# V in its own tile with 320-byte rows and two ones columns, one more free weight buffer: a one-core transformer block

## The chip, the cores and the metric

One core of one Trainium2 chip runs the kernel. The metric is device time in microseconds. Each time quoted is a median of several executions unless it is said otherwise. Ratios with 95% intervals: the mean time of one kernel's fast runs over that of the other's of the same rounds, so not quite the ratio of the medians quoted beside them.

In the profiles TensorE is PE (its weight loads PEld), VectorE is DVE, ScalarE ACT, GpSimd POOL; SP issues transfers. SBUF and PSUM are on-chip memories: this kernel's matmuls read tiles in SBUF and write tiles in PSUM. The granted clock is the share of its full clock that TensorE got, as the trace records it; "half clock" is a record of 0.5.

Below, a "start-to-start" time is the time from the start of one matmul to the start of the next, taken from the starts recorded in the trace. It matters because successive matmuls overlap: in before the profile gives an o_ps 219 ns on average, and the next one starts 57.8 ns after it.

## The reference

A block of 2048 tokens with D = 1024: adaptive layer norm, attention of 32 query heads over 4 cached K/V heads (the last 512 keys of each, head width 128), a residual, adaptive layer norm, a SwiGLU FFN of width 3584, a residual. Cut to what matters here:

```python
W = min(4096, max(256, Sk // 4))                      # 512
k = jnp.repeat(k_cache[:, :, Sk - W:, :], rep, axis=1)
v = jnp.repeat(v_cache[:, :, Sk - W:, :], rep, axis=1)
scores = jnp.einsum('bhqd,bhkd->bhqk', q, k) * Dh ** (-0.5)
p = _softmax(scores, axis=-1)
o = jnp.einsum('bhqk,bhkd->bhqd', p, v)
...
x = x + ga * _A_ref(h, A_k_cache, A_v_cache, A_wq, A_wo)
...
x = x + gb * _B_ref(h, B_w_gate, B_w_up, B_w_down)
```

## The kernel before

V lies in SBUF as 4 heads x 4 key blocks, each block a row of 128 values and some ones behind them. The matmul that makes the attention output reads 129 columns of such a row: 128 of V, and a column of ones whose product is the softmax denominator. A row takes 132 values, so 264 bytes. The tile comes from the pool that also holds wq, wg and wu, and stays there until attention ends.

```python
pa_ = ctx.enter_context(tc.tile_pool(name="blkA", bufs=8))
pb_ = ctx.enter_context(tc.tile_pool(name="blkB", bufs=7))     # wq, wg, wu; before: also kT and V
pc_ = ctx.enter_context(tc.tile_pool(name="blkC", bufs=13))    # wo, wd, oq, oT
# ... cut ...
VW = Dh + 4
v_sb = blkB("v_sb", [P, Hkv, WT, VW])
for kv in range(Hkv):
    load(v_sb[:, kv, :, 0:Dh], v_v[:, kv])
nc.gpsimd.memset(v_sb[:, :, :, Dh:VW], 1.0)
# ... cut ...
def emit_o(g):
    # ... cut ...
    for t in range(QT):
        if o_slot["n"] == 0:
            o_slot["ps"] = mm("o_ps", (P, SLOTS, Dh + 1))
        s_ = o_slot["n"]
        for j in range(WT):
            nc.tensor.matmul(o_slot["ps"][:, s_, :], lhsT=pT[g][:, j, t * P:(t + 1) * P],
                             rhs=v_sb[:, kv, j, 0:Dh + 1], start=(j == 0),
                             stop=(j == WT - 1))
```

There are 128 heads and token chunks, with 16 such matmuls each: 2048 in all. Around them run the 512-column matmuls q_ps (queries), s_ps (scores) and a_ps (output projection). After attention come gu_ps (gate and up) and d_ps (down) of the FFN. Nearly all loads and the transposes by DMA are issued in order from one queue (SP).

Of the kernel before, what the change touches and what calls it, by code (L numbers as in the profile page):

```python
# [11 lines left out]
BF16 = mybir.dt.bfloat16  # L12
# [576 lines left out]
def fast_path(ctx, tc, flag, A_x, A_k_cache, A_v_cache, A_wq, A_wo, B_x, B_w_gate, B_w_up,  # L589
# [3 lines left out]
    nc = tc.nc  # L593
    P = 128
    _, S, D = A_x.shape
    _, Hkv, Sk, Dh = A_k_cache.shape
# [11 lines left out]
    WT = W // P  # L608
# [20 lines left out]
    const = ctx.enter_context(tc.tile_pool(name="const", bufs=1))  # L629
# [1 line left out]
    hpool = ctx.enter_context(tc.tile_pool(name="hT", bufs=4))  # L631
    pa_ = ctx.enter_context(tc.tile_pool(name="blkA", bufs=8))
    pb_ = ctx.enter_context(tc.tile_pool(name="blkB", bufs=7))
    pc_ = ctx.enter_context(tc.tile_pool(name="blkC", bufs=13))
    wk = ctx.enter_context(tc.tile_pool(name="work", bufs=2))
    sm = ctx.enter_context(tc.tile_pool(name="small", bufs=4))
    psp = ctx.enter_context(tc.tile_pool(name="psum", bufs=4, space=bass.MemoryType.PSUM))
# [5 lines left out]
    def blkB(name, shape, dt=BF16):  # L643
        return pb_.tile(shape, dt, name=name, tag="B")

    def blkC(name, shape, dt=BF16):
        return pc_.tile(shape, dt, name=name, tag="C")

    def mm(name, shape=(P, 512), dt=FP32):
        return psp.tile(list(shape), dt, name=name, tag="mm", bufs=4)  # L650
# [15 lines left out]
    def load(out, in_):  # L666
        with nc.allow_non_contiguous_dma(reason="weight slice"):
            fetch(out=out, in_=in_)
# [20 lines left out]
    def load_wq(cc, hg, parts=(0, 1)):  # L689
        for i in parts:  # L690
            t = blkB("wq", [P, 4, 512])
            load(t, wq_v[:, 4 * i:4 * i + 4, hg * 512:(hg + 1) * 512])
            wq_tiles[(cc, hg, i)] = t
# [8 lines left out]
    for kv in range(Hkv):  # L702
        pin(nc.sync.dma_start_transpose(
            out=kT[:, kv, :], in_=A_k_cache[0, kv, k0:k0 + W, :]), "dma")
    VW = Dh + 4
    v_sb = blkB("v_sb", [P, Hkv, WT, VW])
    for kv in range(Hkv):
        load(v_sb[:, kv, :, 0:Dh], v_v[:, kv])
    nc.gpsimd.memset(v_sb[:, :, :, Dh:VW], 1.0)
    load_wq(0, 1)  # L710


# [218 lines left out]
    for half in range(DH):  # L931
# [6 lines left out]
        for n in range(4 * LEAD):  # L938
# [3 lines left out]
                             rhs=hT[("h1", 0)][:, dt, :], start=(dt == 0), stop=(dt == DT - 1))  # L942
# [96 lines left out]
    SLOTS = 3  # L1039
    o_slot = {"n": 0, "runs": []}  # L1040

    def close_bank():
        ps, runs = o_slot["ps"], o_slot["runs"]
        n = o_slot["n"]
        rl = sm.tile([P, SLOTS], FP32, name="rl", tag="rl", bufs=4)
        nc.vector.reciprocal(out=rl[:, 0:n], in_=ps[:, 0:n, Dh])
        for g, t0, t1, s0 in runs:
            cnt = t1 - t0
            dst = oq[(g // H, (g % H) // 4)][:, t0:t1, g % 4, :]
            sc = rl[:, s0:s0 + cnt].unsqueeze(2).to_broadcast([P, cnt, Dh])  # L1050
            nc.vector.tensor_tensor(out=dst, in0=ps[:, s0:s0 + cnt, 0:Dh], in1=sc, op=ALU.mult)  # L1051
        o_slot.update(n=0, runs=[])

    def emit_o(g):
        cc, h = divmod(g, H)
        kv = h // rep
        if h % 4 == 0:
            oq[(cc, h // 4)] = blkC("oq", [P, QT, 4, Dh])
        for t in range(QT):
            if o_slot["n"] == 0:  # L1060
                o_slot["ps"] = mm("o_ps", (P, SLOTS, Dh + 1))
            s_ = o_slot["n"]
            for j in range(WT):
                nc.tensor.matmul(o_slot["ps"][:, s_, :], lhsT=pT[g][:, j, t * P:(t + 1) * P],  # L1064
                                 rhs=v_sb[:, kv, j, 0:Dh + 1], start=(j == 0),
                                 stop=(j == WT - 1))
            runs = o_slot["runs"]
            if runs and runs[-1][0] == g:
                runs[-1][2] = t + 1
            else:  # L1070
                runs.append([g, t, t + 1, s_])
            o_slot["n"] = s_ + 1
            if o_slot["n"] == SLOTS or (t == QT - 1 and h % HQ == HQ - 1):
                close_bank()
        del pT[g]
# [127 lines left out]
    for k in range(NU + 1):  # L1203
        if k % 4 >= 2 and 4 * (k // 4) + 8 < NU:
            g = 4 * (k // 4) + 8
            load_wq(g // H, (g % H) // 4, (k % 4 - 2,))
        if k < NU:
            emit_s(k)
        if k + LEAD < NU:
            emit_q(k + LEAD)  # L1210
        if k == NU - 4:
            load_gu(0, 0)
        run_tasks(k)
        if k >= 1:
            emit_o(k - 1)
# [20 lines left out]
def kernel(tc, *args):  # L1236
    nc = tc.nc
    with tc.tile_pool(name="guard", bufs=1) as gp:
        flag = gp.tile([1, 1], I32, name="flag")
        fast_path(tc, flag, *args)  # L1240
        over = nc.values_load(flag[0:1, 0:1], min_val=0, max_val=1)
        with tc.If(over > 0):
            general_path(tc, *args)
# [30 lines left out]
```

## Time and profile before

| | before |
|---|---|
| time | 1287.03 us, median of 3 (1285.96 to 1289.07) |
| span of the profiled run | 1287.8 us, mean granted clock 0.996 |
| TensorE busy | 1272.8 us, 99% |
| o_ps, sum of start-to-start times | 118.4 us for 2048 matmuls, 57.8 ns each |
| 512-column matmuls, start-to-start | 215 to 216 ns |

From the profile's page of before: the busy times, the granted clock in 40 slices (9 is 90% or more), the chain of waits by engine and by line, and the group of o_ps (busy us and mean ns of one, then idle time before).

```profile
span 1287.8 us, 18140 instructions
...
PE 1272.8 (99%) x7601; PEld 644.0 (50%) x7601; DVE 577.8 (45%) x1271; ACT 334.0 (26%) x433; POOL 1.3 (0%) x8
...
PEclk9999999999999999999999999999999999999999
...
PE 95%; DMA 2%; DVE 1%; SPq 1%; ACT 0%; issue 0%; DVEq 0%
...
L1064 PE MATMUL o_ps<-v_sb,pT 128*128 128x129 bf16 x2048 | 139.2, 219 | 0.0
```

TensorE is the limit, and nearly all of the chain of waits is TensorE's own work. The 139.2 us of the last line is not what o_ps costs, because the runs of o_ps overlap with their neighbours. The timeline of TensorE shows the cost (start, length, count):

```profile
600.48 1.09 PE L1064 MATMUL o_ps<-v_sb,pT 128*128 128x129 bf16 x16
601.41 1.02 PE L1032 MATMUL s_ps<-qT,kT 128*128 128x512 bf16 x4
602.27 1.03 PE L1019 MATMUL q_ps<-hT,wq 128*128 128x512 bf16 x4
```

Sixteen o_ps begin at 600.48 and the next group begins at 601.41: 0.93 us, or 58 ns each. The four s_ps of 512 columns take 0.86 us, or 215 ns each.

Broken down by the key block j, the start-to-start times in the trace are 56.1, 59.9, 55.9 and 59.4 ns for j = 0 to 3.

Three lines of the view of waits matter (total us, times, longest):

```profile
DVE modT L802 <- DMA modT<-row_d: 3.6, 1, 3.6
...
PE gu_ps L1168 <- DMA wu<-in_B_w_up_dram: 2.1, 1, 2.1
...
PE a_ps L1096 <- DVE acc L1102: 1.0, 1, 1.0
```

The first and the third are one story, near 92 us: VectorE stands still until the small modulation transfer lands, so a copy out of PSUM behind it is late, and TensorE waits for that copy. The second is at 756 us, and the timeline shows what follows it:

```profile
755.16 1.03 PE L1168 MATMUL gu_ps<-hT,wu 128*128 128x512 bf16 x4
...
758.26 1.04 PE L1168 MATMUL gu_ps<-hT,wu 128*128 128x512 bf16 x4 [2.08 <-DMA wu<-in_B_w_up_dram]
...
759.14 3.16 PE L1168 MATMUL gu_ps<-hT,wg 128*128 128x512 bf16 x8
```

Eight gu_ps normally take 1.89 us from first start to last end. The eight at 759.14 take 3.16 us. The trace's record of the granted clock gives half clock from 759.6 us for 3.41 us.

### The profile page before, as it was taken

Reading aid. Unit: us, or ns where it says so; the run is one execution under the profiler, and the core shown is the slowest. Engines: PE = TensorE matmul, PEld = TensorE weight load, DVE = VectorE, ACT = ScalarE, POOL = GpSimd, SP = SyncE. Lnnn points to the kernel's source line nnn. Section 1 sums busy time; section 2 is a strip of 40 time slices with the busy share of each in tenths; the row PEclk is TensorE's granted clock in tenths of the full one; section 3 lists DMA queues with packets and bytes.
Section 4 is the critical chain, followed back from the end, with each engine's and each line's share of the span. In section 5 each row is a group of like instructions: output and inputs, shape, how many; then the busy total and the mean of one; then the engine's idle time right before and its main releaser. Section 6 shows DMA issues by size and latency. Waiting matters only on the chain.

```text
span 1287.8 us, 18140 instructions
## 1 busy us (share of the span) xinstructions
PE 1272.8 (99%) x7601; PEld 644.0 (50%) x7601; DVE 577.8 (45%) x1271; ACT 334.0 (26%) x433; POOL 1.3 (0%) x8
## 2 busy tenths in 40 slices
PE   7999999999999999999999999999999999999998
PEld 4555555555555555555554444444444444444444
DVE  4464557866577755576663641221122121222122
ACT  3543334343333433333341111011100111011100
POOL 0000000000000000000000000000000000000000
PEclk9999999999999999999999999999999999999999
DMA  9878465456345654445578475453536445354401
GB/s 295 264 196 221 169 148 171 133 144 203 96 123 156 148 140 147 116 147 131 132 186 257 134 218 171 135 192 132 179 103 219 152 152 175 135 192 132 147 18 34
DMA packets 280107, 204.20 MB, mean 159 GB/s; under 512 B 113865, under 2 KB 273609, under 8 KB 280018
## 3 DMA queue, kind: packets, MB, share of 16 engines
q1 hardware_dynamic: 275106, 198.78, 52.2%
q10 hardware_dynamic: 4912, 4.20, 1.0%
q8 instruction: 61, 1.00, 0.3%
q14 instruction: 28, 0.23, 0.1%
HBM read 174.08 MB, written 4.21 MB: 138 GB/s over the span
## 4 chain that ended last, share of the span: by engine, by line
PE 95%; DMA 2%; DVE 1%; SPq 1%; ACT 0%; issue 0%; DVEq 0%
PE gu_ps L1168 29%; PE a_ps L1096 17%; PE q_ps L1019 17%; PE d_ps L1188 15%; PE o_ps L1064 9%; PE s_ps L1032 8%; DMA wm<-in_w_mod_dram 1%; SPq L664 1%; DMA modT<-row_d 0%; DMA hT<-xn 0%; DMA wu<-in_B_w_up_dram 0%; PE row_ps L779 0%; PE q_ps L940 0%; DVE st L816 0%; SPq L848 0%; ACT pT L1034 0%
## 5 line engine op out<-in xcount | busy, mean ns | idle before, releaser
L1034 ACT ACTIVATE pT<-s_ps 128x1024 bf16<-128x1024 f32 x256 | 248.6, 1020 | 345.4 <-PE s_ps L1032 345.4
L1096 PE MATMUL a_ps<-wo,oT 128*128 128x512 bf16 x1024 | 241.9, 379 | 1.0 <-DVE acc L1102 1.0
L1019 PE MATMUL q_ps<-hT,wq 128*128 128x512 bf16 x1000 | 237.3, 380 | 0.3 <-DVE modT L755 0.3
L1168 PE MATMUL gu_ps<-hT,wu 128*128 128x512 bf16 x896 | 212.3, 380 | 2.1 <-DMA wu<-in_B_w_up_dram 2.1
L1168 PE MATMUL gu_ps<-hT,wg 128*128 128x512 bf16 x896 | 212.9, 381 | 0.0
L1174 DVE TENSOR_TENSOR guT<-gu_ps,sg 128x512 bf16<-128x512 f32 x112 | 77.4, 691 | 285.5 <-ACT sg L1173 285.5
L1173 ACT ACTIVATE sg<-gu_ps 128x512 bf16<-128x512 f32 x112 | 66.9, 597 | 492.6 <-PE gu_ps L1168 492.6
L1188 PE MATMUL d_ps<-wd,guT 128*128 128x512 bf16 (+2 forms) x952 | 194.2, 366 | 0.0
L916 DVE CAST qT<-q_ps 128x512 bf16<-128x512 f32 x128 | 88.2, 690 | 179.0 <-PE q_ps L1019 176.8
L1096 PEld LDWEIGHTS <-oT 128*128 128x128 bf16 x1024 | 99.9, 98 | 122.3 <-issue 2.1
L1019 PEld LDWEIGHTS <-wq 128*128 128x128 bf16 x1000 | 97.9, 98 | 117.9 <-issue 0.5
L1064 PEld LDWEIGHTS <-pT 128*128 128x128 bf16 x2048 | 128.4, 97 | 30.6 <-issue 0.4
L1188 PEld LDWEIGHTS <-guT 128*128 128x128 bf16 x952 | 90.9, 98 | 103.0
L1168 PEld LDWEIGHTS <-wu 128*128 128x128 bf16 x896 | 87.8, 98 | 108.7 <-DMA wu<-in_B_w_up_dram 2.6
L1168 PEld LDWEIGHTS <-wg 128*128 128x128 bf16 x896 | 87.9, 98 | 106.1 <-issue 1.1
L1064 PE MATMUL o_ps<-v_sb,pT 128*128 128x129 bf16 x2048 | 139.2, 219 | 0.0
L1032 PE MATMUL s_ps<-qT,kT 128*128 128x512 bf16 x512 | 131.3, 378 | 0.6 <-ACT pT L1034 0.6
L1051 DVE TENSOR_TENSOR oq<-o_ps,rl 128x256 bf16<-128x256 f32 (+2 forms) x256 | 101.3, 420 | 4.3
L1192 DVE TENSOR_TENSOR f<-d_ps,gb_bc 128x512 f32<-128x512 f32 (+2 forms) x34 | 22.4, 660 | 147.1 <-PE d_ps L1188 147.1
L1104 DVE TENSOR_TENSOR acc<-a_ps,acc 128x512 f32<-128x512 f32 x64 | 44.1, 688 | 40.8 <-PE a_ps L1096 40.8
L1032 PEld LDWEIGHTS <-kT 128*128 128x128 bf16 x512 | 44.7, 97 | 31.9 <-issue 1.3
L816 DVE BATCH_NORM_STATS2 st<-x 128x6 f32<-128x512 bf16 x64 | 41.3, 680 | 2.7 <-DMA x<-in_A_x_dram 2.5
(75 smaller groups left out, 306.7 us busy)
## 6 DMA issues: line engine op xcount, KB each, us to landing
wq<-in_A_wq_dram SPq DMA_DIRECT2D x64, 512.0 KB, 4.8
wo<-in_A_wo_dram SPq DMA_DIRECT2D x64, 512.0 KB, 5.5
wg<-in_B_w_gate_dram SPq DMA_DIRECT2D x56, 512.0 KB, 5.0
wu<-in_B_w_up_dram SPq DMA_DIRECT2D x56, 512.0 KB, 5.6
wd<-in_B_w_down_dram SPq DMA_DIRECT2D x56, 512.0 KB, 7.2
wmr<-in_w_mod_dram SPq DMA_DIRECT2D x8, 1024.0 KB, 8.6
x<-in_A_x_dram SPq DMA_DIRECT2D x16, 256.0 KB, 5.1
wm<-in_w_mod_dram SPq DMA_DIRECT2D x4, 1024.0 KB, 10.7
```

Of the source, the lines that this page charges most:

```text
L916: nc.vector.tensor_copy(out=t, in_=q_ps)
L1019: nc.tensor.matmul(q_ps, lhsT=wq_tiles[(cc, h // 4, dt // 4)][:, dt % 4, (h % 4) * P:(h % 4 + 1) * P], rhs=hT[("h1", cc)][:, dt, :], start ...
L1032: nc.tensor.matmul(s_ps[:, i, :], lhsT=kT[:, kv, j * P:(j + 1) * P], rhs=qT[g], start=True, stop=True)
L1034: nc.scalar.activation(out=p[:, 2 * jj:2 * jj + 2, :], in_=s_ps, func=ACT.Exp, scale=scale)
L1051: nc.vector.tensor_tensor(out=dst, in0=ps[:, s0:s0 + cnt, 0:Dh], in1=sc, op=ALU.mult)
L1064: nc.tensor.matmul(o_slot["ps"][:, s_, :], lhsT=pT[g][:, j, t * P:(t + 1) * P], rhs=v_sb[:, kv, j, 0:Dh + 1], start=(j == 0), stop=(j == W ...
L1096: nc.tensor.matmul(a_ps, lhsT=oT[(cc, 2 * q + i)][:, hh % 4, t * P:(t + 1) * P], rhs=wo_tiles[(cc, q, dh, i)][:, hh % 4, :], start=(hh == ...
L1104: nc.vector.tensor_tensor(out=acc[(cc, t)][:, dsl], in0=a_ps, in1=acc[(cc, t)][:, dsl], op=ALU.add)
L1168: nc.tensor.matmul(ps[:, n, :], lhsT=gu_w[(cc, fg, nm, dt // 4)][:, dt % 4, fi * P:(fi + 1) * P], rhs=hT[("h2", cc)][:, dt, :], start=(dt ...
L1173: nc.scalar.activation(out=g, in_=ps[:, 0, :], func=ACT.Silu)
L1174: nc.vector.tensor_tensor(out=guT[(cc, fg)][:, fi, :], in0=ps[:, 1, :], in1=g, op=ALU.mult)
L1188: nc.tensor.matmul(d_ps, lhsT=guT[(cc, f // 4)][:, f % 4, t * P:(t + 1) * P], rhs=wd_tiles[(cc, dh, f // 4)][:, f % 4, c0:c0 + w], start=( ...
```

## The change

V gets a tile of its own, outside the pool of wq, wg and wu, whose seven buffers are then all for weights and kT. Rows grow from 264 to 320 bytes. The matmul reads 130 columns, the second ones column being unused, so that the count is even. To make room the pool of wo and wd goes from 13 to 12 buffers.

```diff
-    pc_ = ctx.enter_context(tc.tile_pool(name="blkC", bufs=13))
+    pc_ = ctx.enter_context(tc.tile_pool(name="blkC", bufs=12))
 ...
-    VW = Dh + 4
-    v_sb = blkB("v_sb", [P, Hkv, WT, VW])
+    VN = Dh + 2
+    v_sb = const.tile([P, Hkv, WT, Dh + 32], BF16, name="v_sb")
     for kv in range(Hkv):
         load(v_sb[:, kv, :, 0:Dh], v_v[:, kv])
-    nc.gpsimd.memset(v_sb[:, :, :, Dh:VW], 1.0)
+    nc.gpsimd.memset(v_sb[:, :, :, Dh:VN], 1.0)
 ...
-                o_slot["ps"] = mm("o_ps", (P, SLOTS, Dh + 1))
+                o_slot["ps"] = mm("o_ps", (P, SLOTS, VN))
 ...
-                                 rhs=v_sb[:, kv, j, 0:Dh + 1], start=(j == 0),
+                                 rhs=v_sb[:, kv, j, 0:VN], start=(j == 0),
```

## The prediction

> **What bounds the kernel now.** TensorE. The page gives PE 1272.8 us busy of a 1287.8 us span (99%), granted clock 0.9 or more in all 40 slices; the chain that ended last is 95% PE, 9% of it the line of o_ps (attention probabilities times V). By start-to-next-start of successive matmuls in the trace, a 512-column matmul takes 215 to 216 ns everywhere, and the 2048 o_ps matmuls (129 columns) take 118.4 us in all, 57.8 ns each. PE idles at the start (about 30 us), 1.2 us near 92 us, and near 756 us, where gu_ps waits 2.2 us for a wu transfer and then runs some nine matmuls at half rate.
>
> **What I think the change aims at.** The 57.8 ns is a mean of two values. By the key block j (four in each accumulation), the trace has 56.1, 59.9, 55.9 and 59.4 ns for j = 0, 1, 2, 3. V rows are now 264 bytes apart, so odd j start 8 bytes past a multiple of 16, and even j on one. The PSUM slot makes no difference (57.8 in all three). [...] the trace fits a cost of 3.7 ns for a row that starts in mid-line. Rows of 320 bytes[...] take that away.
>
> **Costs.**
> - Removed: 1024 odd-j matmuls x 3.7 ns = 3.8 us.
> - Added: one column in 2048 matmuls. [...]
> - Net: o_ps 57.8 -> 56.4 ns each, 118.4 -> 115.4 us, about -2.9 us, all of it on PE and so on the critical path.
> - Moved: V leaves the wq/wg/wu pool, so during attention wq has six buffers instead of five. No q_ps matmul waits for wq in the trace, so this is worth nothing directly. The other weight pool has 12 instead of 13; wo and wd are loaded far enough ahead. The order of PE's instructions is the same in both; of the transfers, only a few around the start of the FFN move, and the transposes of hT still stand before the late wu, so I expect the 756 us stall to stay.
>
> **Prediction.** 1287.0 - 2.9 = 1284.1 us; range 1281.8 to 1286.6. Chances: faster by over 2% 0.01, within 2% 0.98, slower by over 2% 0.01.
>
> **What would show it.** o_ps start-to-start near 56.4 ns for all four j, no alternation; the o_ps share of the chain about 2.9 us shorter; 512-column matmuls unchanged; the FFN's start about 2.9 us earlier and the FFN's length equal; the waits for wu near 756 us as before.
>
> **What would make it wrong.** If the alternation comes from the odd column count rather than from the start, the gain still comes, by the even count. [...] The stall near 756 us, or the half-clock stretch after it, may fall differently: up to 4 us either way. One buffer less for wo and wd could hold the single in-order load queue and bring a new wait of some us. The three runs of before differ by 3 us, as much as the gain.

The 3.7 ns is an estimate from the trace of before: 59.9 and 59.4 ns for odd j against 56.1 and 55.9 ns for even j. "In mid-line" and "16-byte line" are words for a start off and on a multiple of 16 bytes. That 16 bytes is the step was assumed then; the runs below test it.

## More of the kernel before

One more piece plays a part. A late column of the modulation is fetched by a small transfer, and VectorE adds 1 to it as soon as it is there:

```python
def load_cols(n, k, dst, add_one):
    # ... cut ...
        fetch(out=dst, in_=src)
    if add_one:
        nc.vector.tensor_scalar(out=dst, in0=dst, scalar1=1.0, scalar2=None, op0=ALU.add)
```

The view of stretches, cut at four landmarks: the first o_ps, the 513th (a quarter of attention), the last, and the first d_ps. The length is the first figure after the colon, then busy times by engine, the granted TensorE clock, DMA share and GB/s.

```profile
0.00:31.57 31.57, 24.90 (x229) 12.52 (x230) 14.83 (x46) 12.22 (x20) 1.26 (x8) 0.95 1.02 293
31.57:186.58 155.01, 154.02 (x1133) 84.89 (x1132) 81.77 (x197) 63.98 (x73) 0.00 (x0) 1.00 0.73 206
186.58:677.40 490.82, 490.82 (x3400) 270.72 (x3399) 325.19 (x778) 190.91 (x229) 0.00 (x0) 1.00 0.52 144
677.40:798.81 121.41, 119.33 (x548) 53.63 (x546) 52.32 (x100) 16.12 (x27) 0.00 (x0) 0.99 0.62 189
798.81:1287.83 489.02, 483.77 (x2297) 222.28 (x2295) 103.69 (x153) 50.75 (x85) 0.00 (x0) 1.00 0.43 142
```

In the third stretch TensorE is busy for all of its 490.82 us. The others hold waits.

## The result, and the profile after

| | before | after |
|---|---|---|
| median | 1286.64 us (6 runs, 1285.78 to 1289.07) | 1287.17 us (6 runs, 1284.57 to 1287.59) |
| ratio | | 0.9997, 95% interval 0.9984 to 1.0010 |
| span of the profiled run | 1287.8 us | 1282.7 us |
| o_ps, start-to-start, sum | 118.4 us | 116.1 us |

The times are the same within noise, although the two profiled runs differ by 5.1 us. The six times of after fall into two groups, 1284.6 and 1284.8 us against 1287.1 to 1287.6, and the profile fell on the first. A pair of profiles taken alone would have told a wrong story.

From the page of after, then its view of waits, then the timeline of TensorE at the same place in the program:

```profile
span 1282.7 us, 18139 instructions
...
PE 1269.7 (99%) x7601; PEld 642.9 (50%) x7601; DVE 577.8 (45%) x1271; ACT 333.9 (26%) x433; POOL 1.2 (0%) x8
...
L1064 PE MATMUL o_ps<-v_sb,pT 128*128 128x130 bf16 x2048 | 137.1, 220 | 0.0
```

```profile
DVE modT L802 <- DMA modT<-row_d: 3.4, 1, 3.4
...
PE gu_ps L1168 <- DMA wu<-in_B_w_up_dram: 2.1, 1, 2.1
...
PE a_ps L1096 <- DVE acc L1102: 0.7, 1, 0.7
```

```profile
597.26 1.07 PE L1064 MATMUL o_ps<-v_sb,pT 128*128 128x130 bf16 x16
598.16 1.03 PE L1032 MATMUL s_ps<-qT,kT 128*128 128x512 bf16 x4
```

Sixteen o_ps now take 0.90 us, or 56 ns each. By j, the start-to-start times are 56.7, 56.7, 56.7 and 56.7 ns: the alternation is gone. Note that the group's mean duration on the page rose, from 219 to 220 ns, while the cost fell.

The same five stretches of after:

```profile
0.00:30.37 30.37, 25.43 (x229) 13.56 (x230) 14.84 (x46) 12.23 (x20) 1.23 (x8) 0.94 1.02 287
30.37:184.61 154.24, 153.51 (x1133) 84.43 (x1132) 81.69 (x197) 63.97 (x73) 0.00 (x0) 1.00 0.77 210
184.61:673.91 489.30, 489.30 (x3401) 269.36 (x3399) 325.23 (x778) 190.85 (x229) 0.00 (x0) 1.00 0.55 146
673.91:793.65 119.74, 117.64 (x548) 53.20 (x546) 52.34 (x100) 16.12 (x27) 0.00 (x0) 1.00 0.62 183
793.65:1282.70 489.05, 483.77 (x2297) 222.32 (x2295) 103.72 (x153) 50.75 (x85) 0.00 (x0) 1.00 0.45 143
```

The 5.1 us come from four places: 1.20 us in the start, 0.77 us in the first quarter of attention, 1.52 us in the rest of it, and 1.67 us at the entry to the FFN. Only the third is a stretch without waits in either kernel. In the last of the four, the wait for wu is there as before, but no half clock follows it:

```profile
754.79 1.04 PE L1168 MATMUL gu_ps<-hT,wu 128*128 128x512 bf16 x4 [2.10 <-DMA wu<-in_B_w_up_dram]
...
755.66 0.59 PE L1168 MATMUL gu_ps<-hT,wg 128*128 128x512 bf16 x2
```

The record of the clock in after's trace has one half-clock stretch in the run's body, 14.0 to 17.4 us. It falls on h_ps and warm_ps (eight h_ps took 1.01 us there and 0.62 us at 9.80 us), in front of a wait for modulation weights, which still lasted 0.35 us there, against 1.37 us in before. In before one fell on q_ps (22.3 us) and one on gu_ps (759.6 us).

What decides where the half clock falls is not shown. In before the wait of 2.08 us for wu was followed by half clock 1.3 us after its end; in after the wait of 2.10 us was not. So the length of the wait does not decide it alone in this pair, and no run was made to test what does.

### The profile page after: what moved, and what is told of

Same layout as the page of the kernel before. It is cut to its first block, busy times and chain, and to the rows that moved or that the text cites. A ratio compares the mean times of both kernels' runs of the same rounds, so it can differ in the third digit from the quotient of the medians.

```text
span 1282.7 us, 18139 instructions
## 1 busy us (share of the span) xinstructions
PE 1269.7 (99%) x7601; PEld 642.9 (50%) x7601; DVE 577.8 (45%) x1271; ACT 333.9 (26%) x433; POOL 1.2 (0%) x8
## 4 chain that ended last, share of the span: by engine, by line
PE 95%; DMA 2%; DVE 1%; SPq 1%; ACT 0%; issue 0%; DVEq 0%
PE gu_ps L1168 29%; PE a_ps L1096 17%; PE q_ps L1019 17%; PE d_ps L1188 15%; PE o_ps L1064 9%; PE s_ps L1032 8%; DMA wm<-in_w_mod_dram 1%; SPq L664 1%; DMA hT<-xn 0%; DMA modT<-row_d 0%; DMA wu<-in_B_w_up_dram 0%; PE row_ps L779 0%; PE q_ps L940 0%; DVE st L816 0%; SPq L848 0%; ACT pT L1034 0%
## 5 line engine op out<-in xcount | busy, mean ns | idle before, releaser
L1064 PE MATMUL o_ps<-v_sb,pT 128*128 128x130 bf16 x2048 | 137.1, 220 | 0.0
L1032 PEld LDWEIGHTS <-kT 128*128 128x128 bf16 x512 | 44.9, 98 | 31.7 <-issue 1.3
```

The source lines that it names most:

```text
L1032: nc.tensor.matmul(s_ps[:, i, :], lhsT=kT[:, kv, j * P:(j + 1) * P], rhs=qT[g], start=True, stop=True)
```

## The experiments

Twelve runs. Theory A is that the rows' gain is real and about 2 us, and is hidden by waits on transfers and by where half-clock stretches fall. Theory B is that something in the change, the smaller wo/wd pool above all, takes the gain back. A rival inside theory A is that the odd column count, not the row start, caused the alternation.

This table gathers what the traces gave (us). The columns are: o_ps in all; the time of the first o_ps; the first quarter of attention; the rest of attention; last o_ps to first d_ps.

| run | rows, columns | o_ps | first | quarter | rest | entry |
|---|---|---|---|---|---|---|
| before | 264, 129 | 118.4 | 31.6 | 155.0 | 490.8 | 121.4 |
| after | 320, 130 | 116.1 | 30.4 | 154.2 | 489.3 | 119.7 |
| a1_again | 320, 130 | 116.1 | 31.6 | 155.4 | 489.3 | 119.5 |
| a2_pitch_129 | 320, 129 | 116.1 | 31.5 | 154.9 | 489.3 | 119.4 |
| a3_130_only | 264, 130 | 118.4 | 31.5 | 155.0 | 490.8 | 119.2 |
| a4_pools_only | 264, 129 | 118.4 | 29.6 | 155.1 | 490.8 | 119.5 |
| c1_before_steady | 264, 129 | 118.3 | 31.3 | 155.3 | 490.8 | 118.1 |
| c2_after_steady | 320, 130 | 116.1 | 31.7 | 155.4 | 489.3 | 118.2 |
| e1_after_nowait | 320, 130 | 116.1 | 31.2 | 153.4 | 489.3 | 120.0 |
| e2_before_nowait | 264, 129 | 118.3 | 30.7 | 153.8 | 490.8 | 118.0 |

The fifth stretch, first d_ps to the end, is 488.9 to 489.1 us in all of them. In the first six rows, take TensorE's wait near 92 us (0.7 to 1.9 us) off the quarter: 154.0 us are left in each of the three kernels with 264-byte rows, 153.5 us in each of the three with 320. Take the wait for wu (1.6 to 2.1 us), and in before the 1.7 us lost at half clock, off the entry: 117.6 us are left in all six. So beyond the rows' 2.0 us these profiles differ only in the start, in the two waits and in the half clock.

### The changed kernel again

No edit.

> The changed kernel, unaltered, once more, for the spread. Its six runs fell into two groups (two at 1284.6 to 1284.8 us with a granted clock of 0.998, four at 1287.1 to 1287.6 with 0.995 to 0.997). Theory A (the o_ps gain of 2.3 us is real, and stretches of about 3.4 us of half clock fall either on a wait or on dense matmuls, at the start and after the wait near 752 us): every run with clock 0.998 has a span near 1283, every run with 0.996 near 1285.5, and before, at equal clock, is about 2 to 3 us longer. Theory B (the smaller wo/wd pool gives the gain back): at equal clock, before and after are equal.

Measured: 1286.52 us, median of 5 (1285.13 to 1287.15), ratio 0.9994 with an interval of 0.9981 to 1.0007. The granted clock alone does not sort the runs: 0.998 goes with spans of 1283.4, 1284.8 and 1285.4 us, so theory A in that form is too simple. Its profile shows what else varies. The wait near 92 us was 1.9 us here, against 0.7 in the first profile of the same kernel:

```profile
DVE modT L802 <- DMA modT<-row_d: 4.5, 1, 4.5
...
PE a_ps L1096 <- DVE acc L1102: 1.9, 1, 1.9
```

So the first quarter took 155.4 us, longer than before's 155.0, although its o_ps were faster.

### Padded rows, 129 columns

```diff
-    VN = Dh + 2
+    VN = Dh + 1
```

> The changed kernel with 129 columns in place of 130; 320-byte rows stay. [...] If the odd count is the cause: the alternation returns for odd j, o_ps near 57.8 ns and 118.4 us. Time: [...]after plus 2.3 us.

What was expected if the row start is the cause was no alternation, and a little less time because of one column less.

Measured: o_ps 116.06 us, 56.7 ns for every j. That is the same as with 130 columns to the hundredth of a us. The time was 1286.38 us, median of 6 (1284.65 to 1290.22), ratio 0.9999 (0.9985 to 1.0012). The alternation does not need 130 columns to go away, and the small gain expected for one column less did not come: an odd 129 costs what 130 costs (116.06 us both).

### 264-byte rows, 130 columns

```diff
-                o_slot["ps"] = mm("o_ps", (P, SLOTS, Dh + 1))
+                o_slot["ps"] = mm("o_ps", (P, SLOTS, Dh + 2))
-                                 rhs=v_sb[:, kv, j, 0:Dh + 1], start=(j == 0),
+                                 rhs=v_sb[:, kv, j, 0:Dh + 2], start=(j == 0),
```

> The kernel before with 130 columns only, rows still 264 bytes. Start theory: odd j still 3 to 4 ns slower than even j[...]. Odd-count theory: 56.7 ns for all j, 116.1 us.

Measured: 56.1, 59.9, 55.8 and 59.4 ns for j = 0 to 3, 118.36 us in all, as in before. The time was 1286.65 us, median of 4, ratio 0.9994 (0.9980 to 1.0009). The odd count is refuted as the cause. The second ones column is neither a gain nor a cost, here too (118.36 us with 130 columns and with 129). The view of one line's instructions tells these kernels apart by the shortest duration (min/median/max in ns), first this run, then a2_pitch_129:

```profile
L1064 PE MATMUL o_ps<-v_sb,pT x2048: 217/220/230, 31.5 to 677.3; 128*128 128x130 bf16 x187
```

```profile
L1064 PE MATMUL o_ps<-v_sb,pT x2048: 220/220/231, 31.5 to 675.7; 128*128 128x129 bf16 x187
```

Durations of 217 ns exist, in these runs, only where rows start off a multiple of 16 bytes (264 bytes, and the 258 below); with 272 and 320 bytes the shortest is 220 ns. The costlier stream has the shorter minimum, so this view shows that the two differ, not which is cheaper.

### The buffers alone

```diff
-    pc_ = ctx.enter_context(tc.tile_pool(name="blkC", bufs=13))
+    pc_ = ctx.enter_context(tc.tile_pool(name="blkC", bufs=12))
-    v_sb = blkB("v_sb", [P, Hkv, WT, VW])
+    v_sb = const.tile([P, Hkv, WT, VW], BF16, name="v_sb")
```

> The kernel before with V in its own tile and the wo/wd pool at 12, rows still 264 bytes and 129 columns: the move of the buffers alone. Theory A: o_ps as before (57.8 ns), and no new wait of PE: the time of before at equal clock, within 0.5 us. Theory B (the pool gives back what the rows gain): 2 to 3 us longer than before at equal clock, with a wait of PE for wo, wd or wu that before does not have.

Measured: 1285.68 us, median of 5 (1284.78 to 1286.05), ratio 0.9989 (0.9976 to 1.0002). Theory B wanted this to be 2 to 3 us longer than before; it is not. It came out about 1 us below before, more than the 0.5 us that theory A allowed, though within noise. It also came out 0.8 us below a1_again (1286.52 us), which has the same buffers and padded rows: timings of the kernels as they are do not show the gain of the rows. Its profile has no half clock before the end and the earliest first o_ps of all (29.6 us). Its quarter, rest and entry are those of 264-byte kernels. One short wait of q_ps for wq near 28.7 us (0.52 us) is new.

### The disturbances taken out, first try: a failure

Fillers in the start, the +1 emitted later, pools 8 and 12 (for the changed kernel 8 and 11).

```diff
-        warm(2)
+        warm(6 if t == 1 else 2)
 ...
         mod_cols(1, half, ca1, True)
+        if half == 1:
+            warm2_ps = big("warm2_ps")
+            for _ in range(6):
+                tc.keep_in_program_order(nc.tensor.matmul(
+                    warm2_ps[:, 0, :], lhsT=ones_bf, rhs=warm_w, start=True, stop=True))
         mod_cols(0, half, sa, False)
 ...
-        if add_one:
-            nc.vector.tensor_scalar(out=dst, in0=dst, scalar1=1.0, scalar2=None, op0=ALU.add)
+    def cols_add_one(dst):
+        nc.vector.tensor_scalar(out=dst, in0=dst, scalar1=1.0, scalar2=None, op0=ALU.add)
 ...
+    at(24, cols_add_one, cb1)
 ...
-    pb_ = ctx.enter_context(tc.tile_pool(name="blkB", bufs=7))
+    pb_ = ctx.enter_context(tc.tile_pool(name="blkB", bufs=8))
```

> The kernel before, with the disturbances around it taken out: warm-up matmuls fill TensorE's waits at the start, the +1 that waits for a small transfer is emitted eight steps later (the wait near 92 us), and the wq/wg/wu pool has 8 buffers, the wo/wd pool 12 (the wait near 756 us). Rows of 264 bytes, 129 columns. If half-clock stretches and these waits are what spreads the times: no stretch of half clock after 25 us, no wait over 0.5 us after 32 us, a spread of its runs under 1.5 us, and a time 3 to 5 us below before. If they are not: the time and the spread of before.

> The changed kernel with the same edits (pools 8 and 11). Theory A (the rows' gain is real and was hidden by where stretches of half clock and the wait near 92 us fall): 2.0 us less than the steadied before, from 1.5 us in the last three quarters of attention and 0.5 us in the first. Theory B (something in the changed kernel takes the gain back): the two within 0.7 us of each other.

Measured: 1287.11 us (1286.14 to 1288.06) for the 264-byte one and 1285.65 us (1285.27 to 1286.56) for the padded one, each a median of 5; ratios to before 1.0002 and 0.9991. The difference of the means is 1.3 us in favour of the padded rows, between the two theories. The expected gain over before did not come:

- The +1 still ran in front of the copy out of PSUM, although the program emits it later. In the padded one VectorE still waited 4.28 us for the transfer, and TensorE 1.06 us behind it.
- A new wait appeared near 109 us in both (0.6 us in the view of the padded one).
- The pools did their part: the wait for wu was gone from both, and the entry took 118.1 and 118.2 us. Yet the time of the 264-byte one did not fall.
- The fillers did not start attention earlier: first o_ps at 31.3 and 31.7 us. The last modulation weights arrived at about 21.3 us in the first of them, as late as in after, the rest of the start comes behind that transfer, and q_ps then waited 0.6 us for wq. One of the two still had a half-clock stretch (14.7 to 18.1 us).

### Rows of 258 and of 272 bytes

```diff
-    VW = Dh + 4
+    VW = Dh + 1
```

```diff
-    VW = Dh + 4
+    VW = Dh + 8
```

The second also takes the wo/wd pool to 12.

> The kernel before with rows of 258 bytes (no padding): the 16 V blocks then start 0, 2, 4, 6, 8, 10, 12 or 14 bytes past a multiple of 16. Line theory: only blocks at 0 cost 56.7 ns, the other offsets all cost more, on average 1 to 2 ns. If only an offset of exactly 8 bytes were slow: four of the sixteen blocks slow.

> The kernel before with rows of 272 bytes (a multiple of 16 but not of 32 or 64) in the same pool, wo/wd pool at 12 to make room, 129 columns. If a start on a 16-byte line is enough: 56.7 ns for all j, 116.1 us in all, like rows of 320. If 32 or 64 bytes were needed: odd j slow as before.

One look each (their state is unknown, so only the matmuls' intervals in attention at full clock are used; the times were 1288.71 us for 258 bytes and 1290.56 us for 272, whose trace has two half-clock stretches after the start, from 94.0 and 759.6 us). Rows of 272 bytes: 56.7 ns for every j and 489.3 us for the rest of attention, like 320. So rows on multiples of 16 bytes are enough here. Rows of 258 bytes: o_ps 120.5 us, rest of attention 492.4 us.

The sum of the four start-to-start times of one accumulation orders all the cases:

| where the four rows start, bytes past a multiple of 16 | sum of the four, ns |
|---|---|
| 0, 0, 0, 0 (rows of 272 or 320) | 226.7 |
| 0, 8, 0, 8 (rows of 264) | 231.2 |
| 0, 2, 4, 6 (rows of 258, heads 0 and 2) | 234.7 |
| 8, 10, 12, 14 (rows of 258, heads 1 and 3) | 235.3 |

Part of the expectation failed. The first row of an accumulation showed 56.1 ns in all heads, whether it starts at 0 or at 8. Four rows off a multiple of 16 cost only 0.6 ns more than three (235.3 against 234.7 ns). (The offsets take the tile itself to start on a multiple of 16, which no trace shows.) The number of 16-byte pieces that a row touches is not the cause: the 258 bytes of 129 columns touch 17 from every start in the table. So the time of a single matmul here cannot be blamed on its own row: with 264-byte rows those that start on a multiple of 16 show 56.1 and 55.9 ns, less than the 56.7 ns that they show where all are so placed. We read this as a delay that shifts between neighbours, and trust only sums over a stream. Why it is not proportional stays open.

### The effect made four times as large

```diff
-            for j in range(WT):
+            for j in list(range(WT)) * 4:
```

in both kernels. Each accumulation is made four times and the last one stays, so the result is right.

> The kernel before with every o_ps accumulation made four times over (each time from a fresh start flag, so the result is the same): four times as many reads of V rows, 8192 matmuls. o_ps 57.8 ns each, 473 us in all, about 350 us more than before. It is the partner of the next run.

> The changed kernel with the same fourfold o_ps. Theory A (the rows' gain is real and reaches the time, under a fixed loss of about 1 us in the first 110 us and a spread of 1 us from the start): o_ps 56.7 ns, 464 us; 8 to 9 us less than the fourfold before, a ratio near 0.9945, clear of noise. Theory B (something takes the gain back in proportion, as waits for transfers would): less than 4 us.

Measured: 1639.68 us (1638.58 to 1639.86) and 1633.15 us (1631.72 to 1633.83), medians of 5; ratios to before 1.2739 (1.2721 to 1.2756) and 1.2690 (1.2672 to 1.2707). The intervals do not overlap. The means differ by 6.6 us. o_ps fell from 472.4 to 464.2 us, so by 8.2 us; s_ps grew by 0.3 us; and the wait for wu at the FFN's entry was longer in the padded one's profile. Of each pair of lines below, the first is from the 264-byte kernel, the second from the padded one:

```profile
PE gu_ps L1168 <- DMA wu<-in_B_w_up_dram: 0.7, 1, 0.7
```

```profile
PE gu_ps L1168 <- DMA wu<-in_B_w_up_dram: 1.9, 1, 1.9
```

The two profiled spans differ by 7.7 us: 7.9 us in attention (8.2 - 0.3), 1.2 us in the start, less 1.2 us in that wait and 0.2 us after it. Without the start this is near the 6.6 us of the times, but with one look at each kernel that is no proof. 6.6 us is less than the 8 to 9 us that theory A asked for, and more than the 4 us that theory B allowed. So most of the 7.9 us reaches the time. That the rest was spent in the wait for wu, which belongs to another part of the program, is suggested by this pair and not shown. TensorE has no wait near 92 us in either of these traces, so they say nothing of that one.

### Without the two waits

The +1 moves to an engine that has nothing else to do, and the weight pools are 8 and 11 (8 and 12 with 264-byte rows).

```diff
-            nc.vector.tensor_scalar(out=dst, in0=dst, scalar1=1.0, scalar2=None, op0=ALU.add)
+            nc.gpsimd.tensor_scalar(out=dst, in0=dst, scalar1=1.0, scalar2=None, op0=ALU.add)
 ...
-    pb_ = ctx.enter_context(tc.tile_pool(name="blkB", bufs=7))
-    pc_ = ctx.enter_context(tc.tile_pool(name="blkC", bufs=12))
+    pb_ = ctx.enter_context(tc.tile_pool(name="blkB", bufs=8))
+    pc_ = ctx.enter_context(tc.tile_pool(name="blkC", bufs=11))
```

> The changed kernel with the two other waits taken out and nothing else: the +1 on the late modulation column goes to GpSimd (VectorE then does not wait for that transfer near 92 us), and the pools are 8 and 11 (the wu transfer near 754 us). Should beat both kernels: 1 us from the first wait, 1.5 to 2.2 from the second, and no half-clock stretch after it: 3 to 4 us below after, near 1283 us. If the waits only move elsewhere: within 1 us of after.

> The kernel before with the same two waits taken out (pools 8 and 12), rows of 264 bytes. Theory A: with the wait near 92 us gone, the first quarter of attention gains too, so this is 2.0 us longer than its partner with padded rows (0.5 us in the first quarter, 1.5 in the rest). Theory B: within 0.7 us of it.

Measured: 1283.70 us for padded rows (1283.04 to 1284.57), ratio to before 0.9974 (0.9960 to 0.9988); 1284.37 us for 264-byte rows (1284.01 to 1285.74), ratio 0.9984 (0.9970 to 0.9998). Before was 1286.93 us in these rounds. Both beat before, clear of noise, by about 3 and 2 us. Judged by the ratios to before (0.9974 against 0.9997 and 0.9994), the padded one is 2.6 to 3.0 us below after, at the low edge of the expected 3 to 4. The means of the two differ by 1.0 us, which is again between the theories. The stretches say why. First the 264-byte kernel (quarter, rest, entry), then the padded one:

```profile
30.71:184.55 153.84, 152.78 (x1113) 84.81 (x1132) 81.96 (x196) 63.90 (x73) 0.23 (x1) 1.00 0.75 211
184.55:675.31 490.76, 487.45 (x3338) 270.73 (x3400) 325.37 (x778) 190.92 (x229) 0.00 (x0) 1.00 0.55 145
675.31:793.35 118.04, 117.05 (x537) 53.31 (x546) 52.23 (x100) 16.12 (x27) 0.00 (x0) 1.00 0.62 189
```

```profile
31.16:184.51 153.35, 152.30 (x1113) 84.42 (x1132) 81.83 (x196) 63.88 (x73) 0.23 (x1) 1.00 0.77 210
184.51:673.81 489.30, 485.98 (x3338) 269.38 (x3399) 325.13 (x778) 190.84 (x229) 0.00 (x0) 1.00 0.56 147
673.81:793.85 120.04, 117.22 (x538) 53.32 (x547) 52.25 (x100) 16.12 (x27) 0.00 (x0) 1.00 0.61 178
```

(The smaller counts of TensorE are records missing from the trace.) With the wait near 92 us gone, the first quarter gains the 0.49 us that the rows promise it, and the rest 1.46 us: 1.95 us, as theory A has it. Then the entry to the FFN gives back 2.0 us in this pair of profiles. The timeline of the padded one there has a normalisation on VectorE that waits for a transpose by DMA, and TensorE behind it:

```profile
750.00 0.55 DVE L835 TENSOR_SCALAR xn<-x,mvl 128x1024 bf16<-128x1024 bf16 x1 [5.05 <-DMA hT<-xn]
751.20 1.89 PE L1168 MATMUL gu_ps<-hT,wg 128*128 128x512 bf16 x8 [1.19 <-DVE guT L1174]
```

TensorE waits another 1.05 us at 755.9. In the 264-byte one the same normalisation waited 3.09 us and TensorE lost 0.41 us. The wait for wu is gone from both; the next wait behind it showed up. The 8 and 11 buffers alone do not lengthen that transpose: c2_after_steady has them too, and there the normalisation waited 3.19 us and the entry took 118.2 us. What lengthened it in this one profile stays open.

## Why the prediction was right or wrong

- **TensorE is the limit, and o_ps a 118.4 us part of it.** Right. The stretch without waits shortened by what o_ps and its neighbours saved, to 0.1 us, in every profile.
- **The alternation comes from rows that start off a multiple of 16 bytes.** Right as to what sets it: 264-byte rows kept it with 130 columns (55.8 to 59.9 ns), and 272-byte and 320-byte rows lost it with 129 (56.7 ns for every j). The step of 16 bytes was assumed in the prediction; the 272-byte rows, on multiples of 16 and not of 32, bear it out.
- **"Removed: 1024 odd-j matmuls x 3.7 ns = 3.8 us."** This step was mis-sized. It took the fast half of the alternation (55.9 ns) for the price of a well-placed row. That price is 56.7 ns: after a slow interval (59.9 ns) the next one is short (55.9 ns). The saving is 57.8 - 56.7 = 1.1 ns on all 2048, 2.3 us.
- **"Added: one column in 2048 matmuls."** The charge made for it failed. 129 and 130 columns cost the same with 264-byte rows (118.36 us both) and with 320-byte rows (116.06 us both).
- **Net o_ps -2.9 us.** Measured: -2.3 us in o_ps. The two errors (a saving put 1.5 us too high, a charge of 0.9 us, the 3.8 less the 2.9, for a column that cost nothing) point opposite ways, so that the net was off by only 0.6 us is luck. Of the 2.3 us, 0.3 us comes back in s_ps, so TensorE's stream is 2.0 us shorter. The rest of attention shows three quarters of it, 1.5 us, in all runs with padded rows.
- **"All of it on PE and so on the critical path."** Shown for the rest of attention; it failed to hold for the first quarter as a whole. There a wait ends with the modulation transfer, and its length followed the run (0.7, 1.9 us in two profiles of the same kernel), so the quarter of a1_again was longer than before's, although without the wait it is 0.5 us shorter. The pair without this wait gained the 0.5 us.
- **The wait near 756 us stays.** Right: 2.1 us in both profiles (the prediction's 2.2 us here and 1.2 us near 92 us are slightly misread; the view has 2.1 and 1.0). The warning that the half clock after it may fall differently was right too; it alone is 1.7 us of the 5.1 between the two profiled runs. The half-clock stretches in the body of these two runs are 3.41 us long (from 22.3 and 759.6 us in before, from 14.0 us in after). They fall elsewhere in a1_again, the changed kernel's second profile (from 12.8 and 23.0 us).
- **The pools are worth nothing.** Not contradicted: the buffers alone made no kernel slower (ratio 0.9989, interval 0.9976 to 1.0002).
- **1284.1 us.** Not reached: the medians were 1287.17 and 1286.52 us, where a gain of 2.9 us was forecast. The mean of the six runs, 1286.4 us, was only 0.4 us below before's, 1286.9 us. It lies within the range, but the range's upper end is 0.4 us below the forecast's own starting point, so that bears out no gain. A shorter stream of 2.0 us is less than the spread of one kernel's own times: before ranged over 3.3 us in its first six runs. The intervals of both timings (0.9984 and 0.9981 at their low ends) still hold a gain of 2 us. What is shown is the 1.5 us, stretch by stretch, and 6.6 us when it is made four times as large. Not shown is where the other 1 us or so of the mean went. The start and the two waits can hold it: together they took 32.5 to 34.6 us in the three profiles with 264-byte rows of the table's first six, and 33.2 to 35.3 us in the three with padded rows. But one profile per run is too few to say that the changed kernel draws worse there.

## What to carry to other kernels

Try placing the rows that TensorE streams on multiples of 16 bytes (272 and 320 bytes did here); it cost a few bytes of padding and took 1.1 ns off each matmul of about 130 columns (bf16, rows of 264 bytes before), while 129 columns cost the same as 130. Before counting such a gain, look for the next wait on a transfer downstream, because such a wait can give back what a shorter stretch in front of it gained (1.95 us gained in the last pair's profiles, 2.0 us longer at the entry to the FFN); taking out two such waits (an add on a busy engine, a load behind transposes) gave more here, about 2 us with 264-byte rows, than the rows did, 0.4 us in the means of before and after. When a gain is smaller than the spread of one kernel's times, compare the stretches of the trace that have no waits, and multiply the effect until the clock can see it.
